# Second gated layer of the last pass: seven half-size block products, weights kept as one float32 array and split on load

## The chip, the cores and the metric

The kernel runs on one core of one Trainium2 chip. The metric is the device time of one execution in microseconds (us). TensorE (PE) does matrix products into PSUM, VectorE (DVE) and ScalarE (ACT) do elementwise work, SyncE (SP) issues nearly all DMAs, in the order of its queue. The scheduler of the framework orders each engine's instructions; inside a queue nothing overtakes.

## The reference

```python
# q, k, v: 4 x 12 x 448 x 64, float32
scores = cap * tanh(q @ k.T / sqrt(64) / cap)
attn = softmax(scores) @ v                    # -> x: 1792 tokens x 768
h = x @ w_in1                                 # 768 x 2048
x = (h - tanh(h)) @ w_out1                    # 2048 x 768
h = x @ w_in2
out = (h * sigmoid(1.702 * h)) @ w_out2       # 1792 x 768
```

The weights come in as 64-bit floats. Each factor is used as two float32r parts, a high one and the rest ("split"), and a product is three matmuls: high by high, high by low, low by high.

## The kernel before, in words

Attention for all heads comes first. Then the two layers run in two passes of 896 tokens (`NPASS` = 2, `NT` = 896), so a pass has four stages: `gemm_in(0)`, `gemm_out...`, `gemm_in(1)`, and the output rows. A stage works through 16 or more chunks of weights of 128 x 768 (`chunks`). In the first pass a chunk is converted from 64-bit, split, and both parts are written to DRAM (`kept`); in the second pass both parts are read back (`prepare`, L228 on), two chunks ahead of their use (`LEAD`), into three buffers (`wh_p`). The list `stream` fixes the order of the chunks.

In the last pass two stages already work with seven products of half-size blocks in place of eight (a scheme of Strassen's kind with 7 products, `SEVEN_A` and `SEVEN_B`): `gemm_out_seven` (L738) and `gemm_rows_seven` (L822). Such a stage needs sums of weight blocks (`s1` to `s4`, `t1` to `t4`), made beside the running stage by a generator, `weight_combos` (L276), of which `ahead` (L255) takes some steps per chunk (`rate`); the sums are split and both parts go to DRAM (`keep_split`, L270). It also needs sums of blocks of the left factor; these are made by `right` and `left` and split into eight pairs of buffers (`ring`). The third stage of the last pass, `gemm_in(1)` (L702), is plain: 16 chunks, each by 896 columns in two spans of 512 and 384 columns, 18 matmuls per span. It starts with the last three row blocks of x, since those are ready first. Each span is followed by a tanh and one VectorE instruction (`g_gate`, L629).

"Gate stage" below means this `gemm_in(1)` of the last pass, "out stage" the `gemm_out_seven` before it, "last stage" the `gemm_rows_seven` after it. Where a line is that of a helper: L76 is `hi_act` (the high part, on ACT), L88 `lo_dve` (the low part, on DVE), L241 the reads in `prepare`, L274 the writes in `keep_split`, L756 the adds of the out stage, L932 the writes of the output.

Of the kernel before, what the change touches and what calls it, by code (L numbers as in the profile page):

```python
# [37 lines left out]
def attention_moe_moe(ctx, tc, q, k, v, cap, w_in1, w_out1, w_in2, w_out2, out):  # L38
# [3 lines left out]
    P = 128  # L42
# [143 lines left out]
    def conv_lo(i):  # L186
        h, l = whl[i]
        n = width[i]
        raw_w = raws.pop(i)
        (lo_pool if i in early else lo_dve)(l[:, :n], raw_w[:, :n], h[:, :n])  # L190
        if A0 <= i < A0 + KF:
            nc.sync.dma_start(out=single[i - A0], in_=raw_w)
        if A0 + 2 * KQ <= i < A0 + 3 * KQ:
            return
        for m, t in enumerate((h, l)):
            nc.sync.dma_start(out=kept[i][:, m], in_=t[:, :n].bitcast(F32))
# [12 lines left out]
    KQ = KF // 4  # L209
    A0 = KF  # L210
    R0 = NCH - KF
    SEVEN_A = ("11", "s2", "12", "s3", "s1", "22", "s4")
    SEVEN_B = ("11", "t2", "21", "t3", "t1", "t4", "22")
    block = []
    for base, names in ((A0, ("11", "12", "21", "22")), (R0, ("11", "21", "12", "22"))):
        block.append({m: kept[base + n * KQ:base + (n + 1) * KQ] for n, m in enumerate(names)})
    for m in ("s1", "s2", "s3", "s4"):
        block[0][m] = [dr_p.tile([P, 2, WC], F32, name=f"{m}_{j}") for j in range(KQ)]
        m = m.replace("s", "t")
        block[1][m] = [dr_p.tile([P, 2, WC], F32, name=f"{m}_{j}") for j in range(KQ)]  # L220
    single = [dr_p.tile([P, WC], F32, name=f"single{n}") for n in range(KF)]
    stream = [(kept[i], width[i], chunks[i][3]) for i in range(NCH)] * (NPASS - 1)
    stream += [(kept[i], width[i], chunks[i][3]) for i in range(A0)]
    stream += [(t, WC, HW) for m in SEVEN_A for t in block[0][m]]
    stream += [(kept[i], width[i], chunks[i][3]) for i in range(2 * KF, 3 * KF)]
    stream += [(t, WC, HW) for m in SEVEN_B for t in block[1][m]]

    def prepare(upto):  # L228
        while n_ready[0] <= min(upto, len(stream) - 1):
# [10 lines left out]
            for m, t in enumerate(whl[i]):  # L240
                nc.sync.dma_start(out=t[:, :n].bitcast(F32), in_=src[:, m])  # L241
# [13 lines left out]
    def ahead(i):  # L255
        if not hold[0]:
            prepare(i + LEAD)
        if side:
            due[0] += rate[0]
            while due[0] >= 1:  # L260
                due[0] -= 1
                next(side[0], None)

    def load_sum(dst, src):
        lo = wr_p.tile([P, WC], F32, tag="wr", name="lo")
        nc.sync.dma_start(out=dst, in_=src[:, 0])
        nc.sync.dma_start(out=lo, in_=src[:, 1])
        nc.vector.tensor_tensor(out=dst, in0=dst, in1=lo, op=ALU.add)

    def keep_split(dst, x, hi):  # L270
        hi_act(hi.bitcast(F32R), x)
        nc.vector.tensor_tensor(out=x.bitcast(F32R), in0=x, in1=hi, op=ALU.subtract)
        for m, t in enumerate((hi, x)):
            nc.sync.dma_start(out=dst[:, m], in_=t)  # L274

    def weight_combos(layer):  # L276
        names = (("11", "12", "21", "22"), ("11", "21", "12", "22"))[layer]
        for j in range(KQ):
            slots = []
            for _ in range(2):  # L280
                t = wd_p.tile([P, WC, 2], U32, tag="wd", name="pair").rearrange("p w t -> p (w t)").bitcast(F32)
                slots += [t[:, :WC], t[:, WC:]]
            r = dict(zip(names, slots))
            for n, m in enumerate(names):
                if layer == 0:
                    nc.sync.dma_start(out=r[m], in_=single[n * KQ + j])
                else:
                    load_sum(r[m], block[1][m][j])
                if layer or n % 2:
                    yield  # L290
            first_ = wr_p.tile([P, WC], F32, tag="wr", name="first")
            hi = wr_p.tile([P, WC], F32, tag="wr", name="hi")

            def op(out, a, kind, b):
                nc.vector.tensor_tensor(out=out, in0=a, in1=b, op=kind)

            if layer == 0:
                op(first_, r["21"], ALU.add, r["22"])
                op(r["21"], r["11"], ALU.subtract, r["21"])
                op(r["11"], first_, ALU.subtract, r["11"])  # L300
                op(r["12"], r["12"], ALU.subtract, r["11"])
                made = (("s1", first_, hi), ("s3", r["21"], r["22"]), ("s2", r["11"], None), ("s4", r["12"], None))
            else:
                op(first_, r["12"], ALU.subtract, r["11"])
                op(r["12"], r["22"], ALU.subtract, r["12"])
                op(r["11"], r["12"], ALU.add, r["11"])
                op(r["21"], r["21"], ALU.subtract, r["11"])
                made = (("t2", r["11"], hi), ("t3", r["12"], r["22"]), ("t1", first_, None), ("t4", r["21"], None))
            yield
            for m, x, h in made:  # L310
                keep_split(block[layer][m][j], x, h or wr_p.tile([P, WC], F32, tag="wr", name="hi"))
                yield
# [317 lines left out]
    def g_gate(a, f, ps):  # L630
# [3 lines left out]
        if plain[0]:  # L634
            g = gr[f][:, a]
# [385 lines left out]
```

## Time and profile before

| | us |
|---|---|
| median of 3 runs | 1117.9 (1116.33 to 1118.76) |
| profiled execution | 1118.85 |
| its span in the trace | 1117.1 |
| PE busy | 1104.0 (99% of the span) |
| DVE busy | 769.7 (69%) |
| ACT busy | 643.2 (58%) |
| DMA moved | 261.47 MB, mean 234 GB/s |

The span runs from the first to the last instruction; the execution is 1.75 us longer than its span. The granted TensorE clock is in the top tenth in all 40 slices of the page. A matmul's recorded duration holds the pipeline's depth, so matmuls overlap, and their rate is read from starts.

### The profile page before, as it was taken

What the parts mean: (1) busy time and instruction counts of PE and PEld (TensorE: products, weight loads), DVE (VectorE), ACT (ScalarE), POOL (GpSimd) and SP (SyncE); (2) the same over time, 40 slices, a digit from 0 to 9 for tenths busy, and PEclk for the clock granted to TensorE, in tenths of its full rate; (3) what the DMA queues carried; (4) which work ended last, traced back from release to release, by engine and by line L of the source; (5) the groups of instructions that cost most, each with busy time, mean ns of one, the idle gap of its engine ahead of it and who ended that gap; (6) DMA issues with size and microseconds to landing.
All of it is one profiled execution on the core that took longest, in us unless ns stands there. A gap on an engine that the chain in (4) does not pass through costs nothing.

```text
span 1117.1 us, 16019 instructions
## 1 busy us (share of the span) xinstructions
PE 1104.0 (99%) x5723; PEld 908.8 (81%) x5723; DVE 769.7 (69%) x1157; ACT 643.2 (58%) x916; POOL 59.1 (5%) x56
## 2 busy tenths in 40 slices
PE   8999998999999999999999999999999999999998
PEld 3333332789998888999999999888999889989998
DVE  4788999799994645676654457899976665655341
ACT  6889888899983435666643427777543333213230
POOL 0013344100000000000000000000000000000000
PEclk9999999999999999999999999999999999999999
DMA  6776786464559776656787888878699888639684
GB/s 146 194 211 182 196 245 199 159 198 141 185 184 321 229 268 220 212 210 210 239 257 255 283 278 284 280 269 310 201 332 316 298 271 306 215 111 312 217 283 136
DMA packets 166112, 261.47 MB, mean 234 GB/s; under 512 B 59744, under 2 KB 100240, under 8 KB 166032
## 3 DMA queue, kind: packets, MB, share of 16 engines
q1 hardware_dynamic: 164464, 259.52, 71.4%
q10 hardware_dynamic: 1568, 0.93, 0.3%
q8 instruction: 45, 0.74, 0.3%
q14 instruction: 35, 0.29, 0.1%
HBM read 173.41 MB, written 86.99 MB: 233 GB/s over the span
## 4 chain that ended last, share of the span: by engine, by line
PE 94%; DMA 2%; ACT 2%; SPq 1%; issue 1%; DVE 0%; ACTq 0%
PE ps_h L711 42%; PE ps_o L820 10%; PE ps_y L736 10%; PE ps_y L770 9%; PE ps_o L873 7%; PE ps_pv L428 6%; PE ps_sc L387 5%; PE ps_o L858 1%; PE ps_r L435 1%; PE ps_qk L366 1%; PE ps_tl L397 1%; ACT t L406 1%; PE ps_qk L375 1%; DMA t<-hi 1%; DMA wh<-t 0%
## 5 line engine op out<-in xcount | busy, mean ns | idle before, releaser
L711 PE MATMUL ps_h<-xl,wh 128*128 128x512 f32 (+1 forms) x768 | 280.5, 365 | 0.2 <-DVE xl L88 0.2
L711 PE MATMUL ps_h<-xh,wh 128*128 128x384 f32 (+1 forms) x768 | 278.9, 364 | 0.0
L711 PE MATMUL ps_h<-xh,wl 128*128 128x512 f32 (+1 forms) x768 | 174.7, 362 | 0.0
L711 PEld LDWEIGHTS ps_h<-xl,wh 128*128 128x128 f32 x768 | 144.1, 188 | 17.1 <-DVE xl L88 0.8
L711 PEld LDWEIGHTS ps_h<-xh,wh 128*128 128x128 f32 x768 | 144.0, 188 | 17.1 <-issue 0.7
L711 PEld LDWEIGHTS ps_h<-xh,wl 128*128 128x128 f32 x768 | 139.5, 188 | 16.3 <-issue 1.4
L160 ACT ACTIVATE wr<-wd 128x768 f32<-128x768 f32 x64 | 57.5, 900 | 56.2 <-DVE wl L88 26.6
L406 ACT ACTIVATE t<-ps_sc,tsc 128x896 f32<-128x896 f32 x72 | 69.9, 1007 | 27.4 <-PE ps_sc L387 27.4
L76 ACT CAST rh<-gr 128x448 fp32r<-128x448 f32 (+1 forms) x80 | 43.1, 540 | 72.0 <-PE ps_o L873 39.1
L177 DVE SCALAR_TENSOR_TENSOR wr<-wd,wr 128x768 uint32<-128x768 uint32 x64 | 62.5, 976 | 29.4 <-ACT wd L165 27.0
L633 ACT ACTIVATE g_t<-ps_h 128x512 f32<-128x512 f32 x64 | 35.0, 546 | 72.9 <-PE ps_h L711 72.3
L88 DVE TENSOR_TENSOR rl<-gr,rh 128x448 fp32r<-128x448 f32 (+1 forms) x80 | 47.0, 589 | 43.3 <-ACT rh L76 43.3
L820 PE MATMUL ps_o<-wh,gh 128*128 128x384 f32 x224 | 74.8, 334 | 0.0
L820 PE MATMUL ps_o<-wl,gh 128*128 128x384 f32 x224 | 74.8, 334 | 0.0
L820 PE MATMUL ps_o<-wh,gl 128*128 128x384 f32 x224 | 74.8, 334 | 0.0
L408 ACT ACTIVATE t<-t,cpos 128x896 f32<-128x896 f32 x72 | 72.4, 1043 | 0.4
L88 DVE TENSOR_TENSOR wl<-wr,wh 128x768 fp32r<-128x768 f32 x55 | 52.6, 956 | 28.7 <-ACT wh L76 23.5
L736 PE MATMUL ps_y<-gl,wh 128*128 128x512 f32 (+1 forms) x192 | 69.8, 364 | 0.0
L736 PE MATMUL ps_y<-gh,wh 128*128 128x512 f32 (+1 forms) x192 | 69.7, 363 | 0.0
L387 PE MATMUL ps_sc<-qk 64*128 64x448 f32 x288 | 68.7, 576 | 0.9 <-DVE qk L85 0.8
L428 PE MATMUL ps_pv<-t,rv 128*64 128x448 f32 x288 | 63.7, 548 | 4.0 <-ACT t L406 3.4
L76 ACT CAST wh<-wr 128x768 fp32r<-128x768 f32 x55 | 46.1, 837 | 36.5 <-PE ps_y L736 24.0
(138 smaller groups left out, 2123.6 us busy)
## 6 DMA issues: line engine op xcount, KB each, us to landing
wh<-kept SPq DMA_DIRECT2D x65, 384.0 KB
wl<-kept SPq DMA_DIRECT2D x65, 384.0 KB
wd<-in_moe_w_in_dram SPq DMA_DIRECT2D x64, 384.0 KB
wd<-in_moe_w_out_dram SPq DMA_DIRECT2D x32, 768.0 KB
kept<-wh SPq DMA_DIRECT2D x60, 384.0 KB
kept<-wl SPq DMA_DIRECT2D x60, 384.0 KB
single<-wr SPq DMA_DIRECT2D x16, 384.0 KB
pair<-single SPq DMA_DIRECT2D x16, 384.0 KB
```

The lines of the kernel that those rows point to most:

```text
L76: pin(nc.scalar.copy(out=dst, in_=src))
L88: pin(nc.vector.tensor_tensor(out=dst, in0=src, in1=hi.bitcast(F32), op=ALU.subtract))
L177: pin(nc.vector.scalar_tensor_tensor(out=u, in0=dbls.pop(i)[:, :, 1], scalar=0x80000007, in1=u, op0=ALU.bitwise_and, op1=ALU.bitwise_or))
L387: pin(nc.tensor.matmul(ps[:, j, :S], qk[a, kc], qk[a, :S], start=True, stop=True))
L406: pin(nc.scalar.activation(out=t, in_=ps[:, :, :S], func=AF.Tanh, scale=tsc))
L408: ins = pin(nc.scalar.activation(out=tt[g, c], in_=tt[g, c], func=AF.Exp, scale=cpos))
L428: pin(nc.tensor.matmul(ps[a, :S], w, t[:, j], start=(c == 0), stop=(c == KC - 1)))
L711: pin(nc.tensor.matmul(ps, w[:, kk, :], x[kk][:, a], start=(m == 0), stop=(m == len(seq) - 1)))
L736: nc.tensor.matmul(bank[e][:, :a1 - a0], w[:, kk, c], x[2 * j + kk][:, a0:a1], start=(j == 0 and m == 0), stop=(j == KF // 2 - 1 and m == ...
L770: nc.tensor.matmul(ps[e], w[:, kk, c], x, start=(k == 0 and m == 0), stop=(k == KH - 1 and m == 2))
L820: nc.tensor.matmul(ps[n][:, :HW], g[2 * j + ff][:, a], w[:, ff, :], start=(j == 0 and m == 0), stop=(j == KF // 2 - 1 and m == len(seq) - 1),)
L873: nc.tensor.matmul(ps[n], x[:, t], w[:, kk, :], start=(k == 0 and m == 0), stop=(k == KH - 1 and m == 2),)
```

## The change

1. The gate stage of the last pass becomes `gemm_in_seven`. The weights are cut in two halves of 384 rows and two of 1024 columns, x in two halves of 384 rows and two of 448 tokens. For each of eight steps j there are seven products of nine matmuls of 448 columns, from four chunks: the chunk of the two plain blocks (products 11 and 12), two chunks of sums (`s24`, `s31`: two products each), and half a chunk (product 22). The results are put together with adds on DVE before the tanh.
2. Sums of weights are kept as one float32 array each; the plain blocks of the last stage are kept only so too (`single`). `prepare` reads one array (`fetch`, one chunk further ahead), makes the high part on ACT and the low part on DVE. This holds for `s1` to `s4`, for `s24`, `s31`, and for all 28 chunks of the last stage.
3. The sums for the gate stage (`sums_i`) are made during `gemm_in(0)` and the out stage, those for the last stage (`sums_b`) during the gate stage, into arrays in DRAM of their own (`t1` to `t4`).
4. The out stage's last two products change places (`s4` before `22`), and its end makes the blocks of x that the gate stage needs: after `s4` the sums go into `ring[0..5]`, after `22` the last one into `last_t`.

```diff
@@ conv_lo: what is kept @@
-        if A0 <= i < A0 + KF:
+        if i >= A0:
             nc.sync.dma_start(out=single[i - A0], in_=raw_w)
-        if A0 + 2 * KQ <= i < A0 + 3 * KQ:
+        if A0 + 2 * KQ <= i < A0 + 3 * KQ or i >= R0:
             return
@@ the stream of chunks @@
-    stream += [(t, WC, HW) for m in SEVEN_A for t in block[0][m]]
-    stream += [(kept[i], width[i], chunks[i][3]) for i in range(2 * KF, 3 * KF)]
-    stream += [(t, WC, HW) for m in SEVEN_B for t in block[1][m]]
+    for m in SEVEN_A:
+        stream += [(t, WC, HW) for t in side_a.get(m, unsummed.get(m))]
+    for j in range(KH):
+        ones, sums = kept[I0 + j], [(t, WC, P) for t in side_i[j]]
+        twos = (kept[I0 + KH + j][:, :, HW:], HW, P)
+        if j:
+            stream += [(ones, WC, P), *sums, twos]
...
+    stream += [(t, WC, HW) for m in SEVEN_B for t in side_b[m]]
+    def fetch(i):
+        if NCH <= i < len(stream) and len(stream[i][0].shape) == 2 and i not in whole:
+            whole[i] = wr_p.tile([P, WC], F32, tag="wr", name="whole")
+            nc.sync.dma_start(out=whole[i], in_=stream[i][0])
@@ prepare @@
-            for m, t in enumerate(whl[i]):
-                nc.sync.dma_start(out=t[:, :n].bitcast(F32), in_=src[:, m])
+            fetch(i)
+            if i in whole:
+                x = whole.pop(i)
+                hi_act(whl[i][0], x)
+                lo_dve(whl[i][1], x, whl[i][0])
+            else:
+                for m, t in enumerate(whl[i]):
+                    nc.sync.dma_start(out=t[:, :n].bitcast(F32), in_=src[:, m])
+            fetch(i + 1)
@@ sums for the last stage, made during the gate stage @@
+    def sums_b():
+        for n in range(KH):
...
+            for m, t in r.items():
+                nc.sync.dma_start(out=t, in_=side_b[m][j][:, a])
+            yield
+            yield
+            add(r["22"], r["22"], ALU.subtract, r["12"])
+            add(r["12"], r["12"], ALU.subtract, r["11"])
+            yield
+            add(r["11"], r["22"], ALU.add, r["11"])
+            add(r["21"], r["21"], ALU.subtract, r["11"])
+            for m, t in (("t3", "22"), ("t1", "12"), ("t2", "11"), ("t4", "21")):
+                nc.sync.dma_start(out=side_b[m][j][:, a], in_=r[t])
+            yield
@@ end of the out stage @@
+            if name == "s4":
+                for e in range(3):
+                    add(b11[e], u2[e], ALU.subtract, b11[e])
+                    x_out(e, HI, b11[e])
+                for e in range(3):
+                    add(u2[e], b22[e], ALU.subtract, u2[e])
+                    add(b22[e], b22[e], ALU.subtract, b11[e])
+        for e in range(3):
+            add(b22[e], p1[e], ALU.subtract, b22[e])
+            split(last_t[e], b22[e])
@@ the gate stage @@
+    def gemm_in_seven():
...
+        for j in range(KH):
+            sums = [("s2", "s4"), ("s3", "s1")]
+            for names in [("11", "12"), *sums, ("22",)] if j else [("11",), *sums, ("12",), ("22",)]:
+                i, (wh, wl) = w_next()
+                for n, name in enumerate(names):
+                    ps = ps_next("ps_h")[:, :S]
+                    seq = [
+                        (w[:, 3 * n + kk, :], x[:, :S]) for kk, (h, l) in enumerate(right_of[name])
+                        for w, x in ((wh, h), (wh, l), (wl, h))
+                    ]
...
+                    if name == "11":
+                        p1 = temp("far")
+                        nc.scalar.copy(out=p1, in_=ps)
+                    elif name == "12":
+                        c = temp("v")
+                        add(c, ps, ALU.add, p1)
+                        gate(j, LO, c)
+                    elif name == "s2":
+                        u2 = temp("q")
+                        add(u2, ps, ALU.add, p1)
...
+                    elif name == "s1":
+                        c = temp("v")
+                        add(u4, ps, ALU.add, u4)
+                        gate(j, HI, u4)
+                        add(c, ps, ALU.add, u2)
+                        gate(KH + j, HI, c)
@@ moe, last pass @@
-            side.append(weight_combos(0))
-            rate[0] = 1.75
+            side.extend((sums_a(), sums_i()))
+            rate[0] = 2.25
...
+            side.append(sums_b())
+            rate[0] = 1.0
+            gemm_in_seven()
```

How the instructions move is shown at two places. The first is VectorE where the out stage ends and the gate stage begins. Before, from the adds on the last product (`part`, L756) to the first gates (`gr0`, L636); `xl` and `rl` are low parts of blocks of x and g:

```order
L756 TENSOR_TENSOR part_7719<-ps_y_8240,part_7719 128x448
L756 TENSOR_TENSOR part_7720<-ps_y_8241,part_7720 128x448
L272 TENSOR_TENSOR pair_8318<-pair_8318,hi_8542 128x768
L88 TENSOR_TENSOR xl0_120<-part_7719,xh0_114 128x448
L88 TENSOR_TENSOR xl1_121<-part_7720,xh1_115 128x448
L756 TENSOR_TENSOR part_7721<-ps_y_8242,part_7721 128x448
L88 TENSOR_TENSOR xl2_122<-part_7721,xh2_116 128x448
L636 SCALAR_TENSOR_TENSOR gr0_6209<-g_t_8382,ps_h_8351 128x512
```

In the changed kernel, from the same adds (now L288) to the low part `wl_8426` of the first step's second chunk of sums, read as `whole_8378`:

```order
L288 TENSOR_TENSOR part_7625<-ps_y_8293,part_7625 128x448
L288 TENSOR_TENSOR part_7626<-ps_y_8294,part_7626 128x448
L288 TENSOR_TENSOR part_7627<-ps_y_8295,part_7627 128x448
L88 TENSOR_TENSOR xl3_123<-part_7625,xh3_117 128x448
L288 TENSOR_TENSOR gr5_6262<-part_7625,gr5_6262 128x448
L88 TENSOR_TENSOR xl4_124<-part_7626,xh4_118 128x448
L88 TENSOR_TENSOR xl5_125<-part_7627,xh5_119 128x448
L88 TENSOR_TENSOR rl6_6294<-gr5_6262,rh6_6293 128x448
L288 TENSOR_TENSOR gr6_6263<-part_7626,gr6_6263 128x448
L288 TENSOR_TENSOR gr7_6264<-part_7627,gr7_6264 128x448
L88 TENSOR_TENSOR wl_8426<-whole_8378,wh_8425 128x768
```

Three adds, three low parts of x, four instructions for later blocks of x and then the weights' low part stand in one row, where before the gates followed the low parts of x.

The second is SP's queue in the gate stage. Before, around the reads of two chunks (`kept37`, `kept38`) and the writes of sums (`t3`, `t2`):

```order
L241 DMA wh_8533<-kept37_207 128x768
L241 DMA wl_8534<-kept37_207 128x768
L274 DMA t3_2_256<-pair_8600 128x768
L274 DMA t2_2_248<-hi_8722 128x768
L274 DMA t3_2_256<-pair_8600 128x768
L241 DMA wh_8595<-kept38_208 128x768
L241 DMA wl_8596<-kept38_208 128x768
```

In the changed kernel, from the reads of whole sums for the fifth step (j = 4) to the next step's; `kept43` is half a chunk (product 22 of j = 3), `kept36` the plain blocks of j = 4, `gs` the buffers of `sums_b`:

```order
L241 DMA whole_8878<-s24_4_306 128x768
L241 DMA whole_8916<-s31_4_307 128x768
L262 DMA wh_8843<-kept43_213 128x384
L262 DMA wl_8844<-kept43_213 128x384
L350 DMA t3_2_324<-gs3_6276 128x384
L350 DMA t3_2_324<-gs7_6280 128x384
L350 DMA t1_2_316<-gs2_6275 128x384
L262 DMA wh_8874<-kept36_206 128x768
L262 DMA wl_8875<-kept36_206 128x768
L350 DMA t2_2_320<-gs0_6273 128x384
L350 DMA t4_2_328<-gs1_6274 128x384
```

A chunk's reads still stand behind writes that wait for VectorE's sums; there are more and smaller writes between them.

## Rows read from the trace of the kernel before

**Rows 1.** The page's busy time: us (share of the span) and instructions of each engine.
```profile
PE 1104.0 (99%) x5723; PEld 908.8 (81%) x5723; DVE 769.7 (69%) x1157; ACT 643.2 (58%) x916; POOL 59.1 (5%) x56
```

**Rows 2.** The chain that ended last: start us, us, engine, tile, line.
```profile
436.13 116.27 PE ps_h L711 x576
...
668.88 116.27 PE ps_h L711 x576
785.14 96.73 PE ps_y L770 x468
...
882.80 5.99 DMA t<-hi
888.86 0.85 ACT hi L76
889.73 0.96 DVE pair L272
890.69 0.55 DVE xl L88
891.28 114.87 PE ps_h L711 x568
...
1055.94 4.46 DMA wl<-t
1060.44 19.98 PE ps_o L873 x114
1080.42 5.35 DMA wh<-t
```

**Rows 3.** What PE waited for from 785 us on: us, times, longest.
```profile
PE ps_o L873 <- DMA wh<-t: 2.1, 2, 1.4
PE ps_h L711 <- DVE xl L88: 0.2, 1, 0.2
```

**Rows 4.** The last pass by stage: stretch and its length, then each engine's busy time.
```profile
core 0: us, PE busy (x) PEld busy (x) DVE busy (x) ACT busy (x) POOL busy (x), PEclk, DMA share, GB/s
668.88:785.14 116.26, 116.26 (x577) 104.37 (x577) 104.62 (x173) 85.48 (x145) 0.00 (x0) 1.00 0.82 282
785.14:891.28 106.14, 105.96 (x514) 95.77 (x512) 79.32 (x133) 42.68 (x74) 0.00 (x0) 1.00 0.87 291
891.28:1006.15 114.87, 114.87 (x569) 103.01 (x570) 64.58 (x109) 32.29 (x63) 0.00 (x0) 1.00 0.67 227
1006.15:1113.24 107.09, 104.81 (x600) 103.58 (x599) 43.34 (x83) 27.13 (x54) 0.00 (x0) 1.00 0.74 244
```

**Rows 5.** SP's queue before PE's longer wait: start us, us.
```profile
1050.97 4.45 SPq L932 DMA_DIRECT2D out_dram<-o  x8
1055.52 0.37 SPq L241 DMA_DIRECT2D wh<-t  x1
1055.94 0.46 SPq L241 DMA_DIRECT2D wl<-t  x1
```

**Rows 6.** VectorE groups in the gate stage: busy us, mean ns, idle before.
```profile
L268 DVE TENSOR_TENSOR pair<-pair,lo 128x768 f32<-128x768 f32 x8 | 7.7, 958 | 5.2 <-DMA lo<-kept 4.4 <-issue 0.8
L88 DVE TENSOR_TENSOR restl<-gr,resth 128x128 fp32r<-128x128 f32 x15 | 4.3, 287 | 1.8 <-ACT resth L76 1.8
L693 DVE TENSOR_TENSOR gr<-gr,gr 128x384 f32<-128x384 f32 x7 | 3.9, 559 | 0.2
L88 DVE TENSOR_TENSOR xl<-part,xh 128x448 fp32r<-128x448 f32 x2 | 1.2, 622 | 0.6 <-ACT xh L76 0.6
```

**Rows 7.** VectorE back to back in the out stage: start us, us.
```profile
794.20 0.62 DVE L88 TENSOR_TENSOR rl<-gs,rh 128x448 fp32r<-128x448 f32 x1
794.74 1.16 DVE L673 TENSOR_TENSOR gr<-gr 128x448 f32<-128x448 f32 x2
795.81 0.62 DVE L88 TENSOR_TENSOR rl<-gs,rh 128x448 fp32r<-128x448 f32 x1
```

**Rows 8.** ScalarE groups in the out stage.
```profile
L76 ACT CAST hi<-pair 128x768 fp32r<-128x768 f32 x4 | 3.4, 838 | 12.5 <-DMA t<-hi 12.1 <-DVE pair L295 0.4
L76 ACT CAST xh<-part 128x448 fp32r<-128x448 f32 x11 | 6.0, 564 | 5.3 <-DVE part L756 5.3
```

More of the change, by code (lines that the diff above doesn't have):

```diff
@@ L209, in attention_moe_moe @@
     KQ = KF // 4
+    KH = KF // 2
     A0 = KF
+    I0 = 2 * KF
     R0 = NCH - KF
-    SEVEN_A = ("11", "s2", "12", "s3", "s1", "22", "s4")
+    SEVEN_A = ("11", "s2", "12", "s3", "s1", "s4", "22")
     SEVEN_B = ("11", "t2", "21", "t3", "t1", "t4", "22")
[L214 to L220, printed above, removed]
@@ L261, in ahead @@
                 due[0] -= 1
[L262 to L274, printed above, removed]
@@ new lines, in ahead, with add, four_of_pairs, first_sums @@
+                if side and next(side[0], side) is side:
+                    side.pop(0)
+    def add(out, a, kind, b):
+        nc.vector.tensor_tensor(out=out, in0=a, in1=b, op=kind)
+    def four_of_pairs():
+        slots = []
+        for _ in range(2):
+            t = wd_p.tile([P, WC, 2], U32, tag="wd", name="pair").rearrange("p w t -> p (w t)").bitcast(F32)
+            slots += [t[:, :WC], t[:, WC:]]
+        return slots
+    def first_sums(r11, r12, r21, r22):
+        add(r22, r21, ALU.add, r22)
+        yield "s1", r22
+        add(r21, r11, ALU.subtract, r21)
+        yield "s3", r21
+        add(r11, r22, ALU.subtract, r11)
+        yield "s2", r11
+        add(r12, r12, ALU.subtract, r11)
+        yield "s4", r12
@@ new lines, in attention_moe_moe, with sums_a, sums_i @@
+    done = set()
+    def sums_a():
+        for j in range(KQ):
+            r = four_of_pairs()
+            for n, t in enumerate(r):
+                nc.sync.dma_start(out=t, in_=single[n * KQ + j])
+                if n % 2:
+                    yield
+            for m, t in first_sums(*r):
+                nc.sync.dma_start(out=side_a[m][j], in_=t)
+                yield
+        done.add("a")
+    def sums_i():
+        for j in range(KH):
+            t = wd_p.tile([P, WC, 2], U32, tag="wd", name="pair").rearrange("p w t -> p (w t)").bitcast(F32)
+            r = t[:, :WC], t[:, WC:]
+            for n in range(2):
+                nc.sync.dma_start(out=r[n], in_=single[I0 - A0 + n * KH + j])
+            yield
+            for n, _ in enumerate(first_sums(*(x[:, a:a + HW] for x in r for a in (0, HW)))):
+                if n == 1:
+                    yield
+            for n in range(2):
+                nc.sync.dma_start(out=side_i[j][n], in_=r[n])
+            yield
+        done.add("i")
@@ L314, in attention_moe_moe, with until @@
+    def until(name):
+        while name not in done:
+            if next(side[0], side) is side:
+                side.pop(0)
     NG = B * NP
@@ L633, in g_gate @@
         nc.scalar.activation(out=t, in_=ps, func=AF.Tanh, scale=0.5 * GELU_C)
-        if plain[0]:
-            g = gr[f][:, a]
-            nc.vector.scalar_tensor_tensor(out=g, in0=t, scalar=1.0, in1=ps, op0=ALU.add, op1=ALU.mult)
-            if a.start == 0 and f < KF // 2:
-                late.append(lambda: left(0, f))
-            if a.stop == NT:
-                late.append(lambda: split(rest_g[f], gr[f][:, REST]))
-            return
         g = g_p.tile([P, TC], F32, tag="far", name="g_g")[:, :n]
@@ L706, in gemm_in @@
                 ps = ps_next("ps_h")[:, :a1 - a0]
-                ks = [*range(3, KM), *range(3)] if layer and plain[0] else range(KM)
-                seq = [p for kk in ks for p in ((wh, xh, kk), (wh, xl, kk))]
-                seq += [(wl, xh, kk) for kk in ks]
+                seq = [p for kk in range(KM) for p in ((wh, xh, kk), (wh, xl, kk))]
+                seq += [(wl, xh, kk) for kk in range(KM)]
                 for m, (w, x, kk) in enumerate(seq):
@@ L888, in gemm_rows_seven @@
                     for jj in range(KQ):
[L889 to L890 removed]
+                        nc.sync.dma_start(out=spare[2 * KQ + jj].bitcast(F32)[:, :WC], in_=side_b["12"][jj])
+                if p == 3:
+                    split([t[:, :WC] for t in spare[2 * j:2 * j + 2]], spare[2 * KQ + j].bitcast(F32)[:, :WC])
             for n in range(3):
```

181 lines of the change are left out of this document (96 added, 85 removed).

## The prediction

> **What bounds the kernel now.** I read the busy line first: PE is busy 99% of the span, VectorE 69%, ScalarE 58% [rows 1]. Then the chain of waits that ended last: from the first pass's third stage on it is nearly all PE, each plain stage 116.27 us for 576 matmuls, the out stage 96.73 us for 468 [rows 2]. The few links that are not PE stand at two places: at the start of the gate stage (a write of sums, a high part, a low part, 0.2 us of waiting) and in the last stage, where PE waits twice for a weight chunk to land, 2.1 us together [rows 2, 3]. Last, the windows by stage: PE is busy through all of the gate stage's 114.87 us at a granted clock of 1.00, the higher of the two levels (2.4 GHz), while VectorE has 64.58 us of work there and DMA is busy 0.67 of the time [rows 4]. So PE's columns set the time, and a change pays in full if it removes columns and VectorE and DMA, which get more to do, stay in time.
>
> **Term 1, the matmuls.** The gate stage had 16 chunks of 36 matmuls, 576, in spans of 512 and 384 columns. It gets 8 steps x 7 products x 9 matmuls = 504 of 448 columns. The mean width was the same, so the rate should be near that of a plain stage, 116.27/576 = 0.2019 us, or of 448-column matmuls in the out stage, 96.73/468 = 0.2067 us [rows 2]. The second has the same width and the same change of weights after every matmul, so I take it: 504 x 0.2067 = 104.2 us, and 116.27 - 104.2 = 12.1 us less. By the other rate 101.8 us, 14.5 us less; that is the low end. No other stage's matmul count moves. The clock is 1.00 in all four stages of the last pass [rows 4], and PE is not left idle for longer than now, so I leave it there.
>
> **Term 2, waits that go.** The waits of the last stage, 2.1 us, come where a chunk's two reads stand in SP's queue behind eight output writes that take 4.45 us to issue [rows 5]. Afterwards a chunk is one read of 384 KB instead of two, issued one chunk earlier. A chunk there is 18 matmuls of 384 columns, so that is several us more of lead than the 1.4 us of the longest wait [rows 3]. The 0.2 us at the start of the gate stage goes too: its first product needs only x blocks that are ready before the out stage's last product. I take 2.3 us less; the other end is 0.
>
> **Term 3, waits that come.** Three places.
>
> (a) Start of the gate stage. After the out stage's last product VectorE has ten instructions of 448 columns (three adds, three low parts, four for later blocks) and then the low part of the chunk (s3, s1). Back to back, such instructions start 0.535 us apart though each lasts 0.62 us [rows 7]. With 0.958 us for a 768-wide one and 0.6 us for low parts waiting on their high part [rows 6]: 5.35 + 0.96 + 0.6 = 6.9 us. PE needs it at product s3's third matmul, 29 matmuls on: 6.0 us. So 0.9 us late; without overlap 10 x 0.62 + 0.96 + 0.3 = 7.5, 1.5 us late; if ScalarE stays ahead, 0.
>
> (b) From step 0 to step 1. The chunk of plain blocks is still read as two parts, straight into a buffer of a ring of three. At j = 1 that buffer is freed with 18 matmuls to go, 3.7 us. The transfers on the chain took 4.46, 5.35 and 5.99 us [rows 2], and the second part is issued 0.42 us after the first [rows 5] but is needed two matmuls later. Late by 0.7 at 4.46, 1.6 at 5.35, 2.3 at 5.99. A landing in a quieter stretch may be quicker, so I take 1.0 (0 to 2.3).
>
> (c) The same chunk at j = 2 to 7 has 27 matmuls, 5.58 us for the first part and 5.99 for the second. At 4.46 or 5.35 it is in time; at 5.99 the second part is 0.42 late, six times 2.5 us. I take 1.0 (0 to 2.5).
>
> Sum of term 3: +2.9 (0 to 6.3).
>
> One page rule bears on (b) and (c). The chain's transfers of 384 KB took 4.46 to 5.99 us with others under way [rows 2]. The Trainium skill ("DMA: Bandwidth & Descriptors", section "Anatomy of one DMA — SWDGE (gpsimd) path") gives a fixed 2.0 us and the bytes at 436 GB/s for a transfer issued by GpSimd; that makes 2.9 us, an estimate, and by it (b) and (c) vanish and the sum is 2 us better. These transfers come from another queue and share the engines, and the rows have the say.
>
> **What is costed at nothing, and what hides it.** In the gate stage VectorE gets, by the order, 88 instructions of 448 columns, 50 of 384, 17 of 768 and 16 of 128: by the durations [rows 6] 54.7 + 28.0 + 16.3 + 4.6 = 103.6 us against PE's 104.2; by starts, 0.085 us closer each [rows 7], 89 us. That is 85% of the stage and is hidden, but there is nothing to spare at the single step; if the cover is gone, it is rival A. ScalarE makes the high parts (838 ns each [rows 8]), some 17 x 0.84 us more beside 32.29 us [rows 4]: hidden. In the out stage, by the order's counts, VectorE rises from 79.32 us to some 92, by durations, of 106; in the last stage the low parts are 29 x 0.96 = 28 us more on 43.34, and adds of 384 make some 80 of 105. In `gemm_in(0)`, the fullest with 104.62 us of 116.26 [rows 4], splits go and adds come, within 2 us: no gain, no loss. DMA in the gate stage: about 3.46 MB per step of 13.0 us, 266 GB/s, above its 227 now but below the 282 and 291 that the two stages before it sustain [rows 4]. The first pass has the same PE order and fewer writes of kept parts; the tail behind the last matmul is the same.
>
> **Sum.** -12.1 - 2.3 + 2.9 = -11.5 us. The profiled execution of before took 1118.85 us (span 1117.1 and 1.75 around it), 0.95 above the median of the runs, 1117.9. So 1107.35 for an execution like it, and 1117.9 - 11.5 = 1106.4 for the median. The ends: -14.5 - 2.3 + 0 = -16.8, 1101.1; -12.1 + 0 + 6.3 = -5.8, 1112.1.
>
> **Rivals.**
>
> A. VectorE becomes the bound of the gate stage. For it: the sum of durations is 99% of the stage, uneven over the steps (11 to 14.3 us by the order's counts against PE's 13.0), and VectorE's low parts wait for ScalarE again and again [rows 6]. Against: the starts 0.535 apart [rows 7]. If spacing were by duration, steps would end some 0.7 us late on average, 8 x 0.7 = 5.6 in place of (c)'s 1.0, and (a) 1.5: -12.1 - 2.3 + 5.6 + 1.5 + 1.0 = -6.3, 1111.6 us. The Trainium skill says something like it ("VectorE: DVE Perf Modes", section "The DRAIN you can't avoid"): the next instruction does not start until the pipe is empty, though one that nothing holds starts earlier. By the first half the sum is A's; the trace shows the second for instructions in a row, and no row shows it for chains that alternate with ScalarE. Chance 0.17.
>
> B. SP's queue turns the gate stage into a slower one: the end on the other side. The reads of the plain blocks stand behind the writes of `sums_b`, which wait for VectorE's adds, which wait for reads of their own. If those reads are used before they land, the queue stands still for a landing, 4.46 to 5.99 us [rows 2], and of the plain chunk's slack only 5.58 - 4.46 = 1.1 us covers it: 3.4 to 4.9 us per step, seven times, 24 to 34 us. Instead of (b) and (c): -12.1 - 2.3 + 0.9 + 24 to 34 = +10 to +20, 1128 to 1138 us. It decides from (14.4 - 0.9)/7 = 1.9 us per step on. For it: the order of the queue. Against: two chunks' time lies between reading and adding, over 5.5 us. Chance 0.08.
>
> C. The gain is partly given back in the last stage. There a chunk now takes landing, high part, low part instead of landing alone, and at the end of each product VectorE is busy with the adds. Six such ends, 1 us each (one low part, 0.958 [rows 6]): -11.5 + 6 = -5.5, 1112.4 us. Against: the read is a chunk earlier and VectorE has 25 us free. Chance 0.10.
>
> **Chances.** The forecast's case has 0.65: 1106.4 us, its own range 1101.1 to 1112.1. A and C end inside or just above it. The range that should hold 8 times in 10 is 1101.5 to 1114.5: it leaves out B, the lowest tip and part of A and C where they are worse than worked out. A measurement of this kernel tells differences of about 0.2%, 2.2 us. Faster by more: most of the forecast's case, A and C, 0.87. Slower: B, 0.08. Between, where A and C come together or B is mild: 0.05.
>
> **What the profile will show.** Right: the gate stage is 504 matmuls in 104 to 107 us; PE's waits have no or one short entry in the last stage, one at the third chunk of the gate stage on VectorE's `wl`, and a few on the reads of `kept`; VectorE is busy 89 to 104 us in the gate stage; the clock is 1.00. Term 1 is wrong if 504 matmuls without waits take 101.8 us or less. A shows as PE waiting on `wl` or on adds out of PSUM in most steps; B as waits of 3 us and more on `wh` in every step, with an SP queue that stands before a write; C as waits on `wl` at the product ends of the last stage. A lower granted clock anywhere, or a stage of the first pass that changes its length, would break the sum altogether.

## The result

| | before | after |
|---|---|---|
| median, us (runs of the first comparison) | 1117.16 (4) | 1106.76 (4) |
| the same comparison repeated later | 1117.29 (7) | 1105.32 (4) |
| span in the trace | 1117.1 | 1104.6 |

The ratio is 0.9902 (95% interval 0.9884 to 0.9920), and 0.9888 (0.9865 to 0.9911) in the repetition. The forecast was 1106.4 us, 11.5 less; measured were 10.4 and 12.0 less.

### The profile page after: what moved, and what is told of

Read it like the earlier page. It is cut to its first block, busy times and chain, and to the rows that moved or that the text cites. A ratio compares the mean times of both kernels' runs of the same rounds, so it can differ in the third digit from the quotient of the medians.

```text
span 1104.6 us, 16021 instructions
## 1 busy us (share of the span) xinstructions
PE 1091.8 (99%) x5651; PEld 899.6 (81%) x5651; DVE 837.6 (76%) x1298; ACT 674.9 (61%) x965; POOL 59.0 (5%) x56
## 4 chain that ended last, share of the span: by engine, by line
PE 94%; DMA 2%; ACT 2%; DVE 1%; issue 1%; SPq 0%; DVEq 0%
PE ps_h L746 32%; PE ps_o L930 11%; PE ps_y L771 11%; PE ps_y L804 9%; PE ps_o L981 8%; PE ps_pv L473 7%; PE ps_h L887 6%; PE ps_sc L432 5%; PE ps_o L966 2%; PE ps_qk L411 1%; PE ps_r L480 1%; PE ps_tl L442 1%; ACT t L451 1%; PE ps_qk L420 1%; DMA wh<-kept 1%
## 5 line engine op out<-in xcount | busy, mean ns | idle before, releaser
L746 PE MATMUL ps_h<-xl,wh 128*128 128x384 f32 (+1 forms) x576 | 210.3, 365 | 0.0
L746 PE MATMUL ps_h<-xh,wh 128*128 128x384 f32 (+1 forms) x576 | 209.4, 364 | 0.0
L746 PE MATMUL ps_h<-xh,wl 128*128 128x384 f32 (+1 forms) x576 | 131.1, 362 | 0.0
L746 PEld LDWEIGHTS ps_h<-xh,wh 128*128 128x128 f32 x576 | 108.1, 188 | 12.9 <-issue 0.7
L746 PEld LDWEIGHTS ps_h<-xl,wh 128*128 128x128 f32 x576 | 108.1, 188 | 12.3
L746 PEld LDWEIGHTS ps_h<-xh,wl 128*128 128x128 f32 x576 | 104.6, 188 | 12.6 <-issue 1.4
L76 ACT CAST wh<-whole 128x768 fp32r<-128x768 f32 x60 | 50.0, 833 | 58.1 <-PE ps_h L887 35.2
L76 ACT CAST rh<-gr 128x448 fp32r<-128x448 f32 (+1 forms) x85 | 45.8, 541 | 50.7 <-PE ps_o L981 24.4
L88 DVE TENSOR_TENSOR wl<-whole,wh 128x768 fp32r<-128x768 f32 x60 | 57.2, 953 | 15.1 <-ACT wh L76 14.8
```

The source lines that it names most:

```text
L76: pin(nc.scalar.copy(out=dst, in_=src))
L88: pin(nc.vector.tensor_tensor(out=dst, in0=src, in1=hi.bitcast(F32), op=ALU.subtract))
L746: pin(nc.tensor.matmul(ps, w[:, kk, :], x[kk][:, a], start=(m == 0), stop=(m == len(seq) - 1)))
```

## The profile after

The page's busy line, which answers to [rows 1]: PE has 12.2 us less, VectorE 67.9 us more, and PE still fills 99% of the span.

```profile
PE 1091.8 (99%) x5651; PEld 899.6 (81%) x5651; DVE 837.6 (76%) x1298; ACT 674.9 (61%) x965; POOL 59.0 (5%) x56
```

The last pass by stage, answering to [rows 4] (stretch and length, busy time of PE, weight loads, VectorE, ScalarE, GpSimd, then granted clock, DMA share, GB/s):

```profile
669.51:785.77 116.26, 116.26 (x577) 104.37 (x577) 104.24 (x186) 78.14 (x133) 0.00 (x0) 1.00 0.79 270
785.77:889.93 104.16, 104.16 (x506) 94.62 (x505) 83.57 (x144) 50.75 (x88) 0.00 (x0) 1.00 0.58 189
889.93:996.66 106.73, 103.86 (x505) 94.19 (x505) 93.28 (x175) 44.01 (x82) 0.00 (x0) 1.00 0.80 259
996.66:1100.71 104.05, 104.03 (x601) 103.71 (x599) 77.50 (x134) 50.61 (x88) 0.00 (x0) 1.00 0.40 122
```

The third line is the new gate stage, with VectorE at 93.28 us in place of 64.58 and DMA at 259 GB/s in place of 227; the fourth is the last stage, now without idle time of PE.

The chain that ended last, answering to [rows 2]:

```profile
785.77 104.15 PE ps_y L804 x504
889.93 9.12 PE ps_h L887 x45
899.05 5.96 DMA wh<-kept
905.06 36.91 PE ps_h L887 x180
...
964.64 0.47 DVE gs L288
965.13 0.32 SPq L350
965.55 0.38 SPq L262
...
966.02 5.20 DMA wl<-kept
```

The out stage runs into the gate stage without a break. The chain leaves PE only inside the gate stage: after 45 matmuls for a landing (the time from a transfer's issue until its data are there) of 5.96 us, and later through VectorE's sums, a write in SP's queue and a read behind it. PE's waits from 785 us on, answering to [rows 3], are all on reads of `kept`:

```profile
PE ps_h L887 <- DMA wh<-kept: 2.1, 1, 2.1
PE ps_h L887 <- DMA wl<-kept: 0.7, 3, 0.3
```

This table gives each stage from its first matmul's start to the next stage's (the last stage: to its last matmul's start), worked out from the matmul starts in the traces. The part before `gemm_in(0)` of the last pass ends between 666.5 and 669.5 us over all these traces, also of one and the same kernel; so experiments are compared by stage. The traces show where the difference comes from. In each of the fourteen PE stands still for 2.0 us in the attention, near 190 us. In seven of them, `before` and the first trace of the changed kernel among them, the granted clock falls to 0.50 (1.2 GHz) within 1.5 us after that, for 3.4 us, and the part ends at 668.7 to 669.5 us; in the other seven it stays at 1.00 and the part ends at 666.5 to 668.0 us. These some 2 us of a whole execution belong to no change in the last pass, and the medians of a few runs carry them. Medians are in us; a ratio is to the runs of before on the same chip, and its 95% interval reaches 0.001 to 0.003 to either side.

| kernel | out stage | gate stage | last stage | gemm_in(0) to the end | median (ratio) |
|---|---|---|---|---|---|
| before | 104.15 | 116.85 | 106.89 | 448.35 | 1117.9 |
| changed | 104.15 | 106.73 | 103.85 | 435.30 | 1106.76 (0.9902) |
| changed, repeated | 104.15 | 106.82 | 103.85 | 435.38 | 1105.32 (0.9888) |
| `no_sums` | 104.15 | 104.16 | 103.83 | 432.88 | 1101.70 (0.9853) |
| `before_whole` | 104.15 | 116.32 | 103.93 | 444.87 | 1115.14 (0.9968) |
| `before_out_act` | 104.15 | 117.32 | 105.78 | 448.50 | 1115.31 (0.9979) |
| `no_lead` | 104.15 | 108.57 | 103.83 | 437.09 | 1107.07 (0.9896) |
| `dve_plus2` | 104.15 | 109.53 | 103.83 | 438.07 | 1106.64 (0.9893) |
| `dve_plus4` | 104.15 | 107.32 | 105.85 | 437.87 | 1105.03 (0.9873) |
| `sums_pool` | 103.33 | 113.44 | 103.83 | 441.54 | 1112.31 (0.9943) |
| `plain_whole` | 104.15 | 106.21 | 103.83 | 434.67 | 1104.25 (0.9868) |
| `plain_whole`, repeated | 104.15 | 105.01 | 103.83 | 433.47 | 1102.47 (0.9860) |
| `all_whole` | 104.15 | 106.35 | 103.85 | 435.02 | 1104.79 (0.9880) |
| `stall_out` | 106.31 | 105.93 | 103.85 | 441.17 | 1109.08 (0.9915) |

## The experiments

**Term 1 and the cause of the waits: the last stage's sums left out** (`no_sums`).

```diff
     for n, m in enumerate(("11", "21", "12", "22")):
+        side_b[m] = single[R0 - A0 + n * KQ:R0 - A0 + (n + 1) * KQ]
+    for n, m in enumerate(("t1", "t2", "t3", "t4")):
         side_b[m] = single[R0 - A0 + n * KQ:R0 - A0 + (n + 1) * KQ]
...
     def sums_b():
         for n in range(KH):
-            ...                # all reads, adds and writes; the four yields stay
```

> The changed kernel with the making of the last stage's sums left out: no reads, adds and writes of them in the gate stage (L341, L350), and the last stage reads plain blocks in place of the sums, so its output differs. Theory (the plain chunk's reads land late because of the other transfers, 6 us, and SP's order): landings fall to 3 to 4 us, the wait from step 0 to step 1 falls from 2.1 us to under 0.5 and the waits of the later steps to 0; gate stage 104.2 us, or 102.5 with the quicker rhythm. Rival (the ring's buffers come free too late whatever the load): the wait from step 0 to step 1 stays at 1.5 us or more. By the figures of the Trainium skill (DMA: Bandwidth & Descriptors, Anatomy of one DMA) a transfer of 384 KB takes 2.9 us, an estimate; then no wait is left.

Chain and gate-stage window of this kernel:

```profile
887.28 104.16 PE ps_h L879 x504
```

```profile
887.12:991.28 104.16, 104.16 (x506) 94.61 (x504) 80.30 (x146) 43.61 (x82) 0.00 (x0) 1.00 0.50 163
```

504 matmuls in 104.16 us without a wait: term 1 as forecast (504 x 0.2067). The buffer of the plain chunk still comes free only 18 matmuls, 3.7 us, ahead. SP's rows for the read that step 1 needs, in the changed kernel and here, and the stretch from that read to its first use:

```profile
899.05 0.39 SPq L262 DMA_DIRECT2D wh<-kept  x1
899.05:905.06 6.01, 3.90 (x19) 3.19 (x19) 5.84 (x12) 4.27 (x8) 0.00 (x0) 1.00 0.94 299
...
896.40 0.32 SPq L264 DMA_DIRECT2D wh<-kept  x1
896.40:900.14 3.74, 3.74 (x20) 3.38 (x19) 3.31 (x8) 2.56 (x6) 0.00 (x0) 1.00 0.67 228
```

The read starts 9.28 us after the stage's first matmul in both (889.77 and 887.12), so no order in SP's queue held it back in the changed kernel. What differs is the landing: 5.96 us with DMA busy 0.94 of the time, at most 3.74 us with 0.67. For this wait, the largest, the ring sets the lead and the other transfers the landing. For the shorter waits of the later steps this run does not tell load from order. By the Trainium skill's figures for a transfer that GpSimd issues ("DMA: Bandwidth & Descriptors", section "Anatomy of one DMA — SWDGE (gpsimd) path") a landing of 2.9 us, an estimate, would have left no wait in the changed kernel either; there the landing, of a read issued by SP, was 5.96 us and the wait 2.1.

**SP's order: the sums' transfers on GpSimd's queue** (`sums_pool`).

```diff
     def sums_b():
-                nc.sync.dma_start(out=t, in_=side_b[m][j][:, a])
+                nc.gpsimd.dma_start(out=t, in_=side_b[m][j][:, a])
...
-                nc.sync.dma_start(out=side_b[m][j][:, a], in_=r[t])
+                nc.gpsimd.dma_start(out=side_b[m][j][:, a], in_=r[t])
```

> The reads and writes of the sums that are made in the gate stage (L341, L350) are issued by GpSimd's queue instead of SP's, so that no read of a weight chunk stands behind a write that waits for VectorE. Theory (the chunk's read starts when its buffer is free and then takes 4 to 6 us because of the other transfers): the waits on kept stay, 2 to 3 us together; span within 1 us of 1104.6. Rival B (SP's order delays the reads): the waits shrink to under 1 us and the span falls by 1.5 to 2.8 us.

Its PE waits (us, times, longest):

```profile
PE ps_h L887 <- DMA wh<-kept: 3.3, 2, 2.5
PE ps_h L887 <- DVE wl L88: 1.9, 1, 1.9
...
PE ps_h L887 <- DMA wl<-kept: 0.8, 2, 0.6
```

The waits on `kept` did not fall, 4.1 us in place of 2.8, though no write stands ahead of them in SP's queue any more. The longest now falls on product 22 of step 3: its read was issued at 938.14 us, and PE went on at 945.91, with DMA busy 0.96 of the wait. So order alone does not explain the waits, and rival B's forecast (under 1 us) failed. How much of the short waits order makes stays open, since this run changes more than the order. It is slower altogether (1112.31 us, ratio 0.9943, 0.9923 to 0.9962): a wait on VectorE came, and after the longest break between matmul starts, 2.87 us, the granted clock was 0.50 for 3.4 us, in which nine matmuls were 0.373 us apart. Why VectorE was later with this queue was not followed up.

**Term 2 alone, on the kernel before** (`before_whole`).

```diff
-        block[1][m] = [dr_p.tile([P, 2, WC], F32, name=f"{m}_{j}") ...]
+        block[1][m] = [dr_p.tile([P, WC], F32, name=f"{m}_{j}") ...]
...
     def keep_split(dst, x, hi):
+        if len(dst.shape) == 2:
+            nc.sync.dma_start(out=dst, in_=x)
+            return
...
     def prepare(upto):          # with fetch() as in the change
+            if i in whole:
+                x = whole.pop(i)
+                hi_act(whl[i][0], x)
+                lo_dve(whl[i][1], x, whl[i][0])
```

> The kernel before with one part of the change alone: the sums for the last stage are kept as one float32 array, read one chunk further ahead and split on load; the gate stage stays plain and the plain blocks of the last stage stay two arrays. Theory: the waits of the last stage (three gaps, 2.75 us over the normal spacing) go, the stage falls from 106.9 to about 104 us and nothing else moves: time 0.25% down. Rival C (landing, high part, low part is a longer chain than a landing): PE waits for wl at the products' ends, 1 us each, and the stage stays at 106 to 110 us.

Window of its last stage:

```profile
1006.04:1109.97 103.93, 103.93 (x600) 103.81 (x600) 56.78 (x99) 39.25 (x70) 0.00 (x0) 1.00 0.57 184
```

PE waits nowhere in the last two stages. The last stage falls by 2.96 us, the gate stage by 0.53 (its first wait is gone as well), and the time to a ratio of 0.9968 (0.9956 to 0.9980): 3.6 us. Rival C does not show: landing, high part and low part are in time. The edit changes three things at once: half the bytes per chunk, reads into two buffers of their own (`wraw`) in place of the ring, and the earlier issue.

**Which part of term 2: the outputs' queue, and the lead** (`before_out_act`, `no_lead`).

```diff
-            q = nc.scalar if b0 + NB == B and half and a > n * P else nc.sync
+            q = nc.scalar if b0 + NB == B else nc.sync
```

> The kernel before with all output writes of the last pass issued by ScalarE's queue, so that no read of weights stands behind them. Theory (the reads came late because they stood behind 4.45 us of output writes in SP's queue): the waits of the last stage go, 106.9 to 104 to 104.5 us. Rival (two reads of 384 KB per chunk are too slow for two chunks' time, wherever the writes are issued): 2 us or more of waits stay.

The link of its chain at the wait that is left:

```profile
1080.97 6.10 DMA wh<-t
```

The wait at 1058 us, behind the eight output writes [rows 5], is gone; the one near 1085 us stays, one chunk later, with 6.10 us from issue to landing and no output in SP's queue before it. So one of the two waits came from the queue's order and the other from a landing longer than its lead. The theory was half right. The last stage gave 1.1 us; the waits at the start of the gate stage grew by 0.5.

```diff
-            fetch(i + 1)
```

> The changed kernel without reading a float32 chunk one chunk further ahead: it is read only when its parts are made, two chunks before use. Theory (term 2 rests on the longer lead): in the last stage two chunks are 2 x 18 x 0.1733 = 6.2 us, in which a landing of 3 to 5 us, ScalarE's 0.83 and VectorE's 0.95 us must pass, behind output writes more; the last stage grows from 103.85 by 1 to 4 us, with PE waiting for wl, and the gate stage by 0.5 us per step, 4 us. Rival (one read of half the bytes is enough by itself): both stages stay within 0.5 us.

Window of its last stage, then its PE waits, all in the gate stage:

```profile
998.35:1102.18 103.83, 103.83 (x600) 103.82 (x599) 77.34 (x134) 50.16 (x88) 0.00 (x0) 1.00 0.39 123
```

```profile
PE ps_h L886 <- DMA wh<-kept: 2.2, 2, 1.2
PE ps_h L886 <- DMA wl<-kept: 0.9, 3, 0.4
PE ps_h L886 <- DVE wl L88: 0.4, 1, 0.4
```

The last stage stays at 103.83 us, but that does not show the lead to be worthless, since the edit did not shorten it. A low part and the read that follows it, first in the changed kernel (last stage from 996.50 us), then here (from 998.35 us):

```profile
1039.19 0.96 DVE L88 TENSOR_TENSOR wl<-whole,wh 128x768 fp32r<-128x768 f32 x1 [0.46 <-ACT wh L76]
1040.18 0.32 SPq L241 DMA_DIRECT2D whole<-t  x1
...
1041.03 0.96 DVE L88 TENSOR_TENSOR wl<-whole,wh 128x768 fp32r<-128x768 f32 x1 [0.46 <-ACT wh L76]
1042.01 0.32 SPq L241 DMA_DIRECT2D whole<-t  x1
```

The read starts 43.7 us into the stage in both, 0.03 us after a low part has freed one of the two float32 buffers. Nearly all reads of the stage start so. It is the buffers that decide when a read starts, with the edit and without it. Over the 28 chunks of the last stage, the time from a chunk's first read to its first matmul is 11.1 us on average in the changed kernel and 11.4 here (8.6 at the least in both), against 7.6 in the kernel before (4.0 at the least, behind the output writes). Half the bytes and a longer lead came together, and no run takes them apart. The gate stage is 1.8 us longer than the changed kernel's, in one trace: 1.2 us are longer waits, at the first low part (0.6 us between starts, where the two traces of the changed kernel have none and 0.4) and on `kept`, whose reads this edit does not touch; the rest comes from its last 186 matmuls, which start 0.2067 us apart in place of 0.2027 (the last section is on this). None of it is shown to be the lead.

**VectorE's room: adds done twice** (`dve_plus2`, `dve_plus4`).

```diff
                     elif name == "s2":
                         u2 = temp("q")
                         add(u2, ps, ALU.add, p1)
+                        add(u2, ps, ALU.add, p1)
```

and the same for `s4`; in the second kernel also for 12 and `s1`.

> Two of VectorE's adds per step of the gate stage are done twice with the same result (on products s2 and s4): 16 more instructions of 448 columns. By starts 0.535 us apart 8.6 us more, 93.3 to 101.9 us of the stage's 106.7. Theory: nearly all of it is hidden, span up by 0 to 1.5 us. Rival A (spacing by duration, no room at a step): up by 5 to 10 us.

> Four of VectorE's adds per step of the gate stage are done twice (products 12, s2, s4, s1): 32 more instructions of 448 columns, 17.1 us by starts, VectorE 110.4 us. That is more than the stage's 106.7 us, so VectorE bounds the stage whatever the theory. Theory (starts 0.535 us apart): stage 110 to 113 us, span up by 4 to 7 us. Rival A (spacing by duration 0.62 us): 103.6 + 19.8 = 123 us, span up by 16 us or more.

PE waits of the first on the high parts:

```profile
PE ps_h L887 <- DMA wh<-kept: 3.4, 4, 2.3
```

Windows of the second: gate stage, a stretch of it, and last stage; then the one new wait:

```profile
886.97:994.29 107.32, 104.88 (x506) 95.65 (x504) 97.61 (x184) 42.97 (x80) 0.00 (x0) 0.98 0.78 252
902.12:905.53 3.41, 3.21 (x9) 2.86 (x10) 1.24 (x2) 0.00 (x0) 0.00 (x0) 0.50 0.94 340
994.29:1100.10 105.81, 104.69 (x600) 103.67 (x599) 87.03 (x157) 51.62 (x90) 0.00 (x0) 1.00 0.41 126
```

```profile
PE ps_o L985 <- DVE wl L88: 1.1, 2, 0.7
```

With 32 more instructions VectorE did not bound the gate stage, against both expectations: it was busy 97.61 us there, and what PE did not need at once moved into the last stage, which went from 77.50 to 87.03 us of VectorE and lost 2.0 us. With 16 more, the list has no wait of PE for VectorE in the gate stage (0.15 us between starts at the first low part, where the changed kernel itself differs from run to run), and the stage is 2.8 us longer through more waits on `kept`, 4.5 us in place of 2.8. By stage that is more than the 0 to 1.5 us of the theory; the medians do not show it (1106.64 against 1106.76 us). The cost does not rise with the dose, so no slope is read from it. The second kernel's gate stage also holds some 1.4 us of slower clock: after the wait from step 0 to step 1, 2.54 us between starts, the granted clock was 0.50 for 3.4 us, and matmuls started 0.373 us apart. What falls is rival A: the changed kernel's VectorE has room.

**The plain chunks kept whole too** (`plain_whole`, `all_whole`), and the changed kernel beside them.

```diff
         if j:
-            stream += [(ones, WC, P), *sums, twos]
+            stream += [(single[I0 - A0 + j], WC, P), *sums, twos]
```

> The chunk of plain blocks of steps 1 to 7 is read as one float32 array into a buffer of its own, one chunk earlier, and split on load, as the sums are. Theory (PE's columns set the gate stage, and its only waits are the reads of this chunk, which can start only when a buffer of the ring of three is free): the 2.8 us of PE waits on these reads in the gate stage go, VectorE gets 7 x 0.95 = 6.7 us more (93.3 to 100.0 of some 104 us) and hides it; span 1104.6 to about 1102, time 0.2% down. Rival A (VectorE is at its bound): PE waits for wl or for VectorE's adds in several steps, 1 to 6 us together, and the span is the same or up to 1109. On the side: matmuls of 448 columns start 0.2067 us apart until the 2.1 us stall of the changed kernel and 0.2027 after it. If the stall does that, the stage without it keeps 0.2067 and lasts 104.2 us; if the steps after the first are quicker by themselves, 102.4 us.

> The same kernel as plain_whole, beside the changed kernel on one chip. From the profiles (434.7 us from the start of gemm_in(0) against 435.3): 0.6 us less than the changed kernel; anything within 2 us of it is no difference that these runs can tell.

PE waits in the last three stages, repeated run:

```profile
PE ps_h L887 <- DMA wh<-kept: 0.3, 1, 0.3
PE ps_h L887 <- DMA wl<-kept: 0.2, 1, 0.2
```

The wait from step 0 to step 1 is gone in both profiles. What is left lies later, on the half chunk of product 22 (1.6 us once in the first profile, 0.5 here). It measured 1104.25 us (ratio 0.9868, 0.9849 to 0.9887) and 1102.47 us (0.9860, 0.9838 to 0.9882), beside the latter 1105.32 us for the changed kernel: 2.85 us faster by the medians, with intervals that overlap. By stage it is lower in both traces, 434.67 and 433.47 us against 435.30 and 435.38.

```diff
...
-        ones, sums = kept[I0 + j], ...
-        twos = (kept[I0 + KH + j][:, :, HW:], HW, P)
+        ones, sums = single[I0 - A0 + j], ...
+        twos = (single[I0 - A0 + KH + j][:, HW:], HW, P)
...
```

> Every weight chunk of the gate stage is read as one float32 array into a buffer of its own and split on load, the plain blocks and the half chunks of product 22 too; the split parts of these 16 chunks are no longer written in the first pass. Theory (the waits that are left come from reads that need a buffer of the ring of three, or stand behind one that does): all waits on kept go, the gate stage falls from 106.7 to 104.2 us at 0.2067 us per matmul (102.5 if the quicker rhythm sets in), VectorE has 93.3 + 7 x 0.95 + 10 x 0.55 = 105.5 us, of which some spills into the last stage as with the doubled adds; span from the start of gemm_in(0) 435.3 to 432.5 to 433.5. Rival A (VectorE has no room): PE waits for wl in most steps, the gate stage stays at 106 to 109 us.

Its PE waits in the last four stages:

```profile
PE ps_h L887 <- DVE wl L88: 2.0, 2, 1.6
```

No read is waited for any more, but VectorE's low parts are, twice: 1104.79 us, no better than the changed kernel. Here rival A begins, with 17 more splits.

> The changed kernel once more, beside the others on one chip. Stages as in its first trace to 0.5 us: gate stage 106.7 us, last stage 103.9; the time within 0.3% of 1106.8 us. Its rhythm of matmuls after the first stall of the gate stage is 0.2027 again if the rhythm is settled by the program, or 0.2067 if it falls by chance.

The stages repeat within 0.1 us (table above), though the stalls do not fall alike: the rhythm went from 0.2067 to 0.2027 at a gap of 1.88 us, back at one of 0.66 us and again to 0.2027 at one of 0.41 us. So it is not settled by the program. The first low part was late here by 0.4 us between starts, where the first trace had no wait.

**The rhythm: a stall made on purpose** (`stall_out`).

```diff
...
                 i, (wh, wl) = w_next()
+                if p == 0 and j == 0:
+                    nc.vector.scalar_tensor_tensor(
+                        out=wh[:, 0, :P], in0=last_ps[0][:, :P], scalar=0.0, in1=wh[:, 0, :P].bitcast(F32),
+                        op0=ALU.mult, op1=ALU.add)
```

> The changed kernel with one VectorE instruction that rewrites the first 128 columns of the out stage's first weight chunk with the same values, from the last result of the stage before it, so that PE must wait 1 to 4 us before the out stage. Theory S (a stall changes the rhythm of matmuls and weight loads; operands and other engines do not): after the stall the 448-column matmuls start 0.2027 us apart in place of 0.2067, which gives back 2.0 us of the wait over the out stage. Rival (the rhythm belongs to a stage's operands or to the load on DMA): 0.2067 as in the changed kernel, and the whole wait is added.

The whole edit also keeps the last result of each `gemm_in` stage in `last_ps`. Windows over the stall, after it, and later:

```profile
784.30:788.75 4.45, 0.10 (x1) 0.03 (x1) 4.45 (x10) 2.25 (x4) 0.00 (x0) 0.76 0.83 264
788.75:793.00 4.25, 4.25 (x12) 3.77 (x13) 2.78 (x6) 0.51 (x1) 0.00 (x0) 0.50 0.15 61
793.00:800.00 7.00, 7.00 (x35) 6.36 (x34) 6.51 (x12) 2.50 (x5) 0.00 (x0) 0.97 0.67 237
```

PE stood still for 4.4 us; then the granted clock was 0.50, the lower level of 1.2 GHz, through the 4.25 us of the second window, and the out stage went on at 0.2067 us per matmul. Theory S in its simple form fell: a stall does not always bring the quicker rhythm.

## Why the prediction was right

The sum from the start of `gemm_in(0)` fell by 13.05 us, against 11.5 forecast.

- **Term 1**, -12.1: right. Without stalls the new stage takes 104.16 us (`no_sums`) against 116.27.
- **Term 2**, -2.3: right, too small. The last stage gave 3.04 us and the gate stage's old start 0.58. I had summed the waits as the view lists them [rows 3], which start at a matmul's recorded end; the gaps between starts, over the normal spacing, are 2.75 and 0.58 us. Its reason was half right: only one of the two waits came from the output writes, and the longer lead did come (11.1 us on average in place of 7.6), but from the float32 buffers, since `no_lead` has it too. What it is worth beside the halved bytes is not shown.
- **Term 3**, +2.9: the sum was right (106.73 - 104.16 = +2.57), the pieces were not. (a) cost nothing in the first trace and 0.4 us in the repeated one. VectorE, first trace, in the changed kernel from the out stage's last adds to the low part in question:

```profile
889.19 1.68 DVE L288 TENSOR_TENSOR part<-ps_y,part 128x448 f32<-128x448 f32 x3
890.79 0.61 DVE L88 TENSOR_TENSOR xl<-part,xh 128x448 fp32r<-128x448 f32 x1
891.32 0.62 DVE L288 TENSOR_TENSOR gr<-part,gr 128x448 f32<-128x448 f32 x1
891.86 1.15 DVE L88 TENSOR_TENSOR xl<-part,xh 128x448 fp32r<-128x448 f32 x2
892.93 0.62 DVE L88 TENSOR_TENSOR rl<-gr,rh 128x448 fp32r<-128x448 f32 x1
893.46 1.15 DVE L288 TENSOR_TENSOR gr<-part,gr 128x448 f32<-128x448 f32 x2
894.53 0.95 DVE L88 TENSOR_TENSOR wl<-whole,wh 128x768 fp32r<-128x768 f32 x1
```

It ends at 895.48; PE needs it 29 matmuls after the stage's start at 889.77, at 895.76, so 0.28 us were to spare. The adds began 0.6 us before that start, since the last product's three results end one after another, and no low part waited for its high part. (b) cost 2.27 us between starts, not 1.0: the landing was 5.96 us, at the top of the three that I had, and I had chosen below them. In (c) four shorter gaps, on the chain partly behind a write of sums in SP's queue (966 us above), which is rival B's mechanism at a small part of its price (under 2 us for all of (c), against 24 to 34). All gaps over the normal spacing make 4.3 us; 1.7 came back through a rhythm of the matmuls that I had not foreseen.
- **Luck.** Term 2 was 1.3 us too small and the gaps of term 3 were 1.4 us too small, and these two misses cancel: -12.1 - 3.6 + 4.3 = -11.4. The rhythm then took the sum 1.7 us beyond the forecast. I had also left the clock at 1.00 because PE would not be left idle for longer than now. That was wrong: its longest gap between starts in these stages went from 1.73 to 2.48 us. The clock stayed at 1.00 after it, but in `dve_plus4`, with the same wait at 2.54 us, it fell, at a cost of some 1.4 us.
- **Cover**: VectorE 93.28 us in the gate stage (89 to 104 forecast), DMA 259 GB/s (266), no waits on VectorE in the first trace. Rivals A, B and C did not come at the sizes that I gave them.

## What to carry to other kernels

Where PE is dense, price a stage by its columns at the spacing of a like stage in the same trace, and a read by the longest landing on the chain, not a mean, if its stage will load the DMA more than now. Where a ring's buffer is freed by PE, ask how long before its use that is: here 3.7 us, enough for the landing without the sums' transfers and too little with them. A read into a buffer of its own, split on load, took that wait away for 0.95 us of VectorE per chunk (`plain_whole`), until VectorE itself was late (`all_whole`). Measure a wait between the starts of matmuls: here 2.75 us where the list gave 2.1. And whether an edit took away what it was meant to take away is seen in its trace alone (`no_lead`).

## What the runs showed of the hardware

Matmuls of 448 columns run in two rhythms at a granted clock of 1.00. Starts in the changed kernel before and after the first stall:

```profile
901.34 0.37 PE L887 MATMUL ps_h<-rh,wl 128*128 128x448 f32 x1
901.55 0.37 PE L887 MATMUL ps_h<-rh,wh 128*128 128x448 f32 x1
...
905.06 0.47 PE L887 MATMUL ps_h<-xh,wh 128*128 128x448 f32 x1 [2.11 <-DMA wh<-kept]
...
906.60 0.36 PE L887 MATMUL ps_h<-xl,wh 128*128 128x448 f32 x1
906.79 0.37 PE L887 MATMUL ps_h<-xh,wl 128*128 128x448 f32 x1
```

The mean spacing is 0.2067 us until the stall and 0.2027 after it. Where nothing stalls it stays 0.2067 (`no_sums`, both stages). It changes in either direction, nearly always at a stall: in `sums_pool` a gap of 0.62 us in the out stage brought 0.2027 and made the stage 0.8 us shorter than without a gap; in `plain_whole` a gap of 1.97 us brought 0.2027 and one of 0.42 us 0.2067 again. But in `dve_plus4` it went from 0.2067 to 0.2027 at 917.3 us, after the third matmul of step 2, with no gap over 0.21 us near it. And not every stall changes it: a gap of 1.43 us in the gate stage of `stall_out` left it at 0.2067. What picks the rhythm stays open.

In the last pass the granted clock fell to 0.50 at gaps between matmul starts of 2.54 us (`dve_plus4`), 2.87 us (`sums_pool`) and 4.45 us (`stall_out`), and stayed at 1.00 at 2.48 us (the changed kernel) and 2.63 us (`dve_plus2`). At 0.50, matmuls of 448 columns started 0.373 us apart. So a longer gap did not always bring the fall, and after one and the same gap of 2.0 us in the attention it came in seven traces of fourteen. These runs do not show what decides it.
